# Loading q and k of three start-up tiles by heads, in 2-KB rows, and turning them with 64x64 products

## The chip, the cores and the metric

The kernel runs on one core of a Trainium2 chip. The core has a matrix engine (PE in the rows; its weight loads stand apart as PEld), a vector engine (DVE), a scalar engine (ACT), GpSimd (POOL) and SyncE (SP), which here only issues transfers. Sixteen DMA engines move the data of all transfers. The metric is the device time of one execution in microseconds; lower is better.

## The reference, cut to what matters

```python
def _attn_ref(q, k, v):                       # each (8, 8, 576, 64): batch, head, token, dim
    chunk = 64                                # attention within chunks of 64 tokens
    scores = scale * np.matmul(q_c, k_c.transpose(0, 1, 2, 4, 3))
    scores = scores - np.max(scores, axis=-1, keepdims=True)
    attn = np.exp(scores)
    attn = attn / (np.sum(attn, axis=-1, keepdims=True) + 1e-09)
    return np.matmul(attn, v_c)
...
def _moe_ref(x, w_in, w_out, g_ln):           # x: 4608 tokens x 512 (8 heads x 64)
    h = x @ w_in                              # 512 x 1024
    e = np.exp(h - np.max(h, axis=-1, keepdims=True))
    solu = h * (e / (np.sum(e, axis=-1, keepdims=True) + 1e-09))
    ln = (solu - mean) / np.sqrt(var + 1e-06) * g_ln
    return (ln @ w_out).astype(np.float32)    # 1024 x 512
```

The weights come as 8-byte numbers; q, k and v are 4-byte. A token of one head is 64 numbers, 256 bytes, and eight tokens of one head that follow each other lie together in memory (2 KB).

## The kernel before, in words

The 4608 tokens are cut into 36 tiles of 128 tokens (two chunks of 64). For each tile the kernel needs q and k turned, so that the 64 dims of a head lie on partitions: the tiles qT and kT, each 128 partitions (two heads x 64 dims) by four head pairs by 128 tokens. From them PE makes the scores (sx), DVE subtracts the maximum (s_nmax, then e), ACT takes the exponential, DVE sums and divides (s_sum, s_rinv, s_e), the result is turned (attn_t) and multiplied with v. That gives x, already turned, and x goes as a high and a low part (x_h, x_l) into the first product (ph, 24 products of 512 columns), through the softmax and the normalisation (z), and as z_h and z_l into the second product (po, 24 more).

From tile 5 on the tiles run through a loop that is the same for each. Before it stands a start-up whose order is written out by hand, in the table `START` (lines 18 to 31). Each word is a step of a tile or of a piece of weight: `n:1` loads q and k of tile 1, `N:1:0` and `N:1:1` turn its q and its k (the first time the word stands the products are issued, the second time the copy out of PSUM), `S:1` makes its scores, `P:1` loads weight piece 1 (1 MB), `c`, `b`, `C`, `t` and `d` convert a weight piece from 8-byte numbers to a high and a low part on POOL, DVE and ACT, and `w:6` puts six products with the identity on PE, whose results nobody reads. Each engine takes its instructions in the order in which the words stand. `MOVED` says which copies go to DVE and which conversions to POOL; the copies of the turned q and k of tiles 1 to 3 are on ACT.

Tiles 0 to 8 are loaded by `load_natural` (line 317) into the buffer `nat`, which has two places; tile i uses place i % 2. A token lies on a partition and its eight heads side by side. `turn_natural` (line 333) turns a tile with four 128x128 transposes for q and four for k, each taking two heads. All these loads, and the loads of the weights and of v, are issued by SP on one queue. Up to eight are under way, since an issue waits for the one eight places before it, and a load into `nat` also waits until PE has turned the tile that lay in that place.

Of the kernel before, what the change touches and what calls it, by code (L numbers as in the profile page):

```python
# [62 lines left out]
def chunk_attention_then_solu_ffn(  # L63
# [12 lines left out]
    B, H, S, D = q.shape  # L76
    DM, FF = H * D, g_ln.shape[0]
    P = 128
    CH = 64
    NCH = S // CH  # L80
    HP = H // 2
# [25 lines left out]
    def po():  # L107
# [10 lines left out]
    pe, dve, act, pool, sync = (  # L118
        order.engine(e)
        for e in (nc.tensor, nc.vector, nc.scalar, nc.gpsimd, nc.sync)  # L120
    )
# [3 lines left out]
    def evict(word, to, of):  # L125
        if word in moved:
            dve.tensor_copy(out=to, in_=of)
        else:
            act.copy(to, of)

    def bank():
        return ps_t.tile([P, FF // 2], F32, name="tp")

    ident = const.tile([P, P], F32, name="ident")
# [111 lines left out]
    QT, KT, V, QS, KS = {}, {}, {}, {}, {}  # L246
# [19 lines left out]
    def qk_tiles(i):  # L266
        QT[i] = work.tile([P, HP, P], F32, name="qT")
        KT[i] = work.tile([P, HP, P], F32, name="kT")
# [19 lines left out]
    def chunk_of(i, c):  # L288
        n = 2 * i + c
        return n // NCH, n % NCH  # L290
# [17 lines left out]
    nat = work.tile([P, 2, 2, H, D], F32, name="nat", tag="z_t")  # L308

    def tile_parts(i):  # L310

        (b0, n0), (b1, n1) = chunk_of(i, 0), chunk_of(i, 1)
        if b0 == b1:
            return [(0, P, b0, n0 * CH)]
        return [(0, CH, b0, n0 * CH), (CH, P, b1, n1 * CH)]

    def load_natural(i):

        for x, src in enumerate((q, k)):
            for p0, p1, b, s in tile_parts(i):  # L320
                sync.dma_start(
                    nat[p0:p1, i % 2, x],
                    src[b, :, s:s + p1 - p0, :].rearrange("h t d -> t h d"),
                )
# [8 lines left out]
    def turn_natural(i, x):  # L333
        if i not in QT:
            qk_tiles(i)
        t = nat[:, i % 2, x]
        pt = bank().rearrange("p (a t) -> p a t", t=P)
        for hp in range(HP):
            pe.transpose(
                pt[:, hp, :],  # L340
                t[:, 2 * hp:2 * hp + 2, :].rearrange("p a d -> p (a d)"),
                ident,
            )
        yield
        evict(f"N:{i}:{x}", (QT, KT)[x][i], pt)
# [8 lines left out]
    def attn(i):  # L354
        return sy if order.on and i % 2 else sx
# [20 lines left out]
    def softmax_a(i):  # L376
        sv = attn(i)[:, :, 0].rearrange("p j a k -> p a j k")
        nmax = small.tile([P, HP, 2], F32, name="s_nmax")
        dve.tensor_reduce(
            out=nmax, in_=sv, axis=AX.X, op=ALU.max, negate=True  # L380
        )
        e = ES[i % 2][:, :, :CH]
        dve.tensor_tensor(
            out=e.rearrange("p (a j) k -> p a j k", j=2), in0=sv,
            in1=nmax.unsqueeze(3).to_broadcast([P, HP, 2, CH]), op=ALU.add,
        )
        st[i, "e"] = e
# [80 lines left out]
    def start_softmax(i):  # L468
        softmax_a(i)
        yield  # L470
        softmax_e(i)
# [270 lines left out]
    def warm(n):  # L742
# [6 lines left out]

    todo = {  # L750
        "P": load_pair, "n": load_natural,
        "v": load_v, "g": load_g, "Q": load_batch, "q": load_some,
        "G": scale_g, "N": turn_natural, "S": scores, "A": start_softmax, "B": softmax_b,
        "T": attn_transpose, "U": attn_turn, "V": start_values, "c": unit_scale,
        "b": unit_bits, "C": unit_join, "t": unit_high, "d": unit_low, "M": ffn_in, "X": solu_a, "Y": solu_b,
# [19 lines left out]
    for i in range(first, NT):  # L775
# [36 lines left out]
        if odd:  # L812
            if i + 3 < NT:
                softmax_a(i + 3)
                softmax_e(i + 3)
            if i + 1 < NT:
                x_high(i + 1)
        elif i + 1 < NT:
            x_low(i + 1)
# [25 lines left out]
        if odd and i + 4 < NT:  # L845
            softmax_a(i + 4)
# [34 lines left out]
```

## Time and profile before

| | us |
|---|---|
| median of 3 runs | 472.41 (471.82 to 473.7) |
| the profiled execution: time | 473.01 |
| the profiled execution: span of its instructions | 471.2 |

| engine | busy, share of the span |
|---|---|
| PE | 98% |
| PE weight loads | 81% |
| DVE | 79% |
| ACT | 54% |
| POOL | 31% |

A share of the whole span is a mean over two different stretches. The start-up takes about 88 us of the 471; the loop takes the rest. So each stretch is read by itself: first a table of busy times by stretch, then each engine's instructions in order of time. In these, an instruction that stood idle before it has the idle time and what ended it in brackets, and an instruction without brackets followed the one before it on its engine without a gap.

### The profile page before, as it was taken

To read this page: it belongs to the slowest core of one execution; us is meant where nothing else is said; L and a number is where in the kernel's file an instruction comes from. 1 tells how busy PE (TensorE), PEld (TensorE's weight loads), DVE (VectorE), ACT (ScalarE), POOL (GpSimd) and SP (SyncE) were. 2 spreads that over 40 slices of the span, in tenths; PEclk is the share of its full clock that TensorE was granted. 3 is DMA by queue.
4 is the path that set the end of the run, shared out by engine and by line. 5 is a ranking of instruction groups with operands and counts; after the bars stand their busy time and mean duration, and the time that the engine had idled before them with its cause. 6 is when DMAs were issued, how large, how long until landed. Compare 5 with 4: busy or idle time off the path is not lost.

```text
span 471.2 us, 11062 instructions
## 1 busy us (share of the span) xinstructions
PE 461.9 (98%) x4212; PEld 380.9 (81%) x4212; DVE 374.1 (79%) x521; ACT 256.4 (54%) x422; POOL 147.6 (31%) x298
## 2 busy tenths in 40 slices
PE   8999999999999999999999999999999999999997
PEld 6677778788888888888888888888888888888886
DVE  3999999797869887878788878797979797954441
ACT  2979984555544646464645455554555554545451
POOL 2212716151505050505050505042514141424430
PEclk9999999999999999999999999999999999999999
DMA  9999999878786878687258496948743535343231
GB/s 244 313 278 217 216 138 179 176 184 150 194 140 170 154 181 162 167 154 177 70 144 167 134 175 157 180 126 173 160 112 105 121 91 136 85 118 96 73 95 50
DMA packets 192924, 72.57 MB, mean 154 GB/s; under 512 B 177188, under 2 KB 177960, under 8 KB 191976
## 3 DMA queue, kind: packets, MB, share of 16 engines
q1 hardware_dynamic: 186200, 58.89, 57.3%
q0 software_dynamic: 6528, 12.86, 10.3%
q8 instruction: 33, 0.54, 0.5%
q14 instruction: 19, 0.16, 0.1%
q10 hardware_dynamic: 144, 0.13, 0.1%
HBM read 36.70 MB, written 9.44 MB: 98 GB/s over the span
## 4 chain that ended last, share of the span: by engine, by line
PE 85%; DMA 5%; DVE 3%; ACT 3%; SPq 2%; issue 1%; DVEq 0%; ACTq 0%
PE po L54 39%; PE ph L54 37%; PE tp L54 5%; PE sx L54 4%; SPq L54 2%; DMA nat<-in_q_dram 2%; DMA v_sb<-in_v_dram 2%; ACT z L54 1%; DMA attn_t<-a_b 1%; ACT attn_t L54 1%; ACT wo_h L54 1%; DVE z_b L54 1%; DVE z L54 0%; DVE s_sum L54 0%; ACT sq L54 0%
## 5 line engine op out<-in xcount | busy, mean ns | idle before, releaser
L54 ACT ACTIVATE z<-ph,h_nmax 128x1024 f32<-128x1024 f32 x36 | 40.2, 1118 | 139.1 <-DVE h_nmax L54 139.1
L54 PE MATMUL po<-wo_l,z_h 128*128 128x512 f32 (+1 forms) x288 | 113.0, 392 | 0.0
L54 PE MATMUL ph<-wi_l,x_h 128*128 128x512 f32 x288 | 112.8, 392 | 0.0
L54 PE MATMUL ph<-wi_h,x_h 128*128 128x512 f32 x288 | 112.2, 389 | 0.0
L54 PE MATMUL po<-wo_h,z_l 128*128 128x512 f32 (+1 forms) x288 | 111.6, 388 | 0.0
L54 PE MATMUL po<-wo_h,z_h 128*128 128x512 f32 (+1 forms) x288 | 111.4, 387 | 0.0
L54 POOL DMA_DIRECT2D z_t<-z_b x144 | 71.8, 506 | 27.0 <-DVE z_b L54 21.9
L54 PE MATMUL ph<-wi_h,x_l 128*128 128x512 f32 x288 | 78.1, 390 | 0.0
L54 POOL TENSOR_TENSOR u<-ssq,eps 128x1 f32<-128x1 f32 x36 | 6.8, 189 | 213.3 <-ACT sq L54 213.1
L54 DVE TENSOR_REDUCE h_nmax<-ph 128x1 f32<-128x1024 f32 x36 | 44.0, 1222 | 31.3 <-PE ph L54 31.2
L54 PEld LDWEIGHTS ph<-wi_h,x_l 128*128 128x128 f32 x288 | 53.9, 188 | 11.6 <-DVE x_l L54 0.4
L54 PEld LDWEIGHTS po<-wo_l,z_h 128*128 128x128 f32 x288 | 54.1, 188 | 11.4
L54 PEld LDWEIGHTS ph<-wi_l,x_h 128*128 128x128 f32 x288 | 54.1, 188 | 11.5 <-ACT x_h L54 0.2
L54 PEld LDWEIGHTS po<-wo_h,z_l 128*128 128x128 f32 x288 | 54.1, 188 | 11.1
L54 PEld LDWEIGHTS ph<-wi_h,x_h 128*128 128x128 f32 x288 | 54.1, 188 | 11.0
L54 PEld LDWEIGHTS po<-wo_h,z_h 128*128 128x128 f32 x288 | 54.1, 188 | 10.5
L54 DVE TENSOR_TENSOR z_l<-z_t,z_h 128x1024 fp32r<-128x1024 f32 (+1 forms) x37 | 42.0, 1136 | 20.9 <-ACT z_h L54 17.7
L54 DVE SCALAR_TENSOR_TENSOR z<-ph,z 128x1024 f32<-128x1024 f32 x36 | 44.1, 1224 | 13.3 <-ACT z L54 13.2
L54 ACT ACTIVATE z<-z,z_sum 128x1024 f32<-128x1024 f32 x33 | 38.1, 1155 | 22.9 <-DVE z L54 21.7
L54 DVE STREAM_TRANSPOSE z_b<-z 128x1024 f32<-128x1024 f32 x34 | 41.2, 1212 | 7.2 <-DMA v_sb<-in_v_dram 3.3
L54 ACT CAST z_h<-z_t 128x1024 fp32r<-128x1024 f32 (+1 forms) x37 | 36.0, 972 | 8.5 <-PE po L54 4.9
L54 ACT ACTIVATE o_sb<-po,r 128x512 f32<-128x512 f32 (+1 forms) x36 | 24.3, 674 | 24.7 <-POOL r L54 18.6
(76 smaller groups left out, 589.8 us busy)
## 6 DMA issues: line engine op xcount, KB each, us to landing
out_dram<-o_sb SPq DMA_DIRECT2D x35, 256.0 KB, 2.5
v_sb<-in_v_dram SPq DMA_DIRECT2D x32, 256.0 KB, 4.3
z_t<-z_b POOLq DMA_DIRECT2D x128, 64.0 KB, 2.8
z_t<-z_b SPq DMA_DIRECT2D x128, 64.0 KB, 3.0
q_st<-in_q_dram SPq DMA_DIRECT2D x96, 72.0 KB, 3.3
k_st<-in_k_dram SPq DMA_DIRECT2D x96, 72.0 KB, 3.1
w_raw<-in_moe_w_out_dram SPq DMA_DIRECT2D x4, 1024.0 KB, 7.5
attn_t<-a_b POOLq DMA_DIRECT2D x60, 64.0 KB, 3.8
```

The source lines that it names most:

```text
L54: ins = make(*args, **kwargs)
```

## The change

q and k of tiles 1, 2 and 3 are loaded another way. A partition now takes eight tokens of one head, which are 2 KB in one piece: partition 16h + g has tokens 8g to 8g + 7 of head h. The source of the load is walked as 8 heads of 16 rows of 512 numbers; before it was walked as 128 tokens of 8 heads of 64 numbers. A load is 128 rows of 2 KB, before 1024 rows of 256 bytes.

The turn becomes sixteen 64x64 products with the identity for q and sixteen for k. A product takes one of the eight token places of four heads (64 partitions). Its result is 64 dims by 64 columns (four heads x 16 groups of eight tokens), and the copy out of PSUM puts the columns back into the order of the tokens: it reads the eight tokens of a group 64 numbers apart. Row half j of head pair a now has head 4j + a, before 2a + j, and the subtraction that writes e puts the heads back in order.

```diff
+    BY_HEADS = (1, 2, 3)
+
     def load_natural(i):
 
+        if i in BY_HEADS:
+            (_, _, b, s), = tile_parts(i)
+            for x, src in enumerate((q, k)):
+                sync.dma_start(
+                    nat[:, i % 2, x].rearrange("p h d -> p (h d)"),
+                    src[b, :, s:s + P, :].rearrange("h (g t) d -> h g (t d)", t=8),
+                )
+            return
...
         t = nat[:, i % 2, x]
+        if i in BY_HEADS:
+            pt = bank()
+            for y in range(8):
+                for j in range(2):
+                    half = slice(j * D, (j + 1) * D)
+                    pe.matmul(
+                        pt[half, y * D:(y + 1) * D], t[half, y, :], ident[half, half],
+                        start=True, stop=True,
+                    )
+            yield
+            evict(
+                f"N:{i}:{x}", (QT, KT)[x][i].rearrange("p a (g t) -> p a g t", t=8),
+                pt.rearrange("p (t a g) -> p a g t", t=8, a=HP),
+            )
+            return
...
-            out=e.rearrange("p (a j) k -> p a j k", j=2), in0=sv,
+            out=e.rearrange(
+                "p (j a) k -> p a j k" if i in BY_HEADS else "p (a j) k -> p a j k", j=2
+            ),
+            in0=sv,
```

On SP, at the start of the program, the order of the loads is as follows (nat is the buffer of q and k, w_raw a weight piece; the numbers are the shape of the destination):

```order
 L54 DMA g_in<-in_moe_g_ln_dram 4x256
 L54 DMA w_raw<-in_moe_w_in_dram 128x1024 x2
-L54 DMA nat<-in_q_dram 128x8x64
-L54 DMA nat<-in_k_dram 128x8x64
+L54 DMA nat<-in_q_dram 128x1x512
+L54 DMA nat<-in_k_dram 128x1x512
 L54 DMA w_raw<-in_moe_w_in_dram 128x2048
 L54 DMA v_sb<-in_v_dram 128x8x64
 L54 DMA w_raw<-in_moe_w_in_dram 128x2048
```

No load moves in the order; the two of tile 1 change shape, and so do those of tiles 2 and 3 behind them.

On PE, the turns of tile 1 stand between products with the identity (ph<-ident), ahead of the scores of tile 1 (sx<-kT,qT):

```order
 L54 MATMUL ph<-ident 128x256 x3
-L54 MATMUL tp<-ident,nat 128x128 x4
+L54 MATMUL tp<-ident,nat 64x64 x16
 L54 MATMUL ph<-ident 128x256
-L54 MATMUL tp<-ident,nat 128x128 x4
+L54 MATMUL tp<-ident,nat 64x64 x16
 L54 MATMUL ph<-ident 128x256
 L54 MATMUL sx<-kT,qT 64x64 x16
```

Here too nothing moves; each group of four becomes sixteen in its place. The order on DVE, ACT and POOL is the same as before.

## Rows read from the trace of the kernel before

**Rows 1.** Busy us by stretch: PE, PEld, DVE, ACT, POOL; clock, DMA share, GB/s.
```profile
18.00:24.00 6.00, 5.58 (x59) 4.21 (x58) 5.90 (x10) 5.44 (x9) 1.88 (x2) 1.00 1.04 284
24.00:30.00 6.00, 5.71 (x63) 4.43 (x62) 5.90 (x9) 4.88 (x8) 0.28 (x1) 1.00 0.96 219
30.00:54.00 24.00, 23.47 (x299) 19.20 (x298) 23.25 (x34) 20.55 (x41) 9.90 (x7) 1.00 0.97 261
54.00:78.00 24.00, 23.33 (x195) 18.77 (x196) 23.09 (x33) 16.22 (x30) 9.87 (x16) 1.00 1.05 143
...
100.00:460.00 360.00, 360.00 (x3183) 298.14 (x3182) 285.94 (x397) 185.70 (x299) 113.54 (x244) 1.00 0.62 140
```

**Rows 2.** The chain that ended last, in order of time: start, length, what.
```profile
9.84 9.55 DMA nat<-in_q_dram
...
19.43 0.66 PE tp L54 x4
```

**Rows 3.** DVE in order of time: start, length, instruction, idle before and its end.
```profile
13.59 0.69 DVE L54 TENSOR_REDUCE s_nmax<-sx 128x8 f32<-128x512 f32 x1 [0.52 <-PE sx L54]
...
21.83 1.22 DVE L54 SCALAR_TENSOR_TENSOR w_a<-w_a,w_b 128x1024 uint32<-128x1024 uint32 x1
22.97 0.69 DVE L54 TENSOR_REDUCE s_nmax<-sx 128x8 f32<-128x512 f32 x1
...
28.74 0.68 DVE L54 TENSOR_REDUCE s_nmax<-sx 128x8 f32<-128x512 f32 x1
...
53.80 0.69 DVE L54 TENSOR_REDUCE s_nmax<-sx 128x8 f32<-128x512 f32 x1 [0.44 <-ACT x_h L54]
...
65.09 1.22 DVE L54 SCALAR_TENSOR_TENSOR z<-ph,z 128x1024 f32<-128x1024 f32 x1 [0.51 <-ACT z L54]
```

**Rows 4.** ACT in order of time, start-up.
```profile
10.75 1.06 ACT L54 ACTIVATE w_a<-w_a 128x1024 f32<-128x1024 f32 x1 [0.95 <-POOL w_a L54]
11.72 0.57 ACT L54 COPY qT<-tp 128x512 f32<-128x512 f32 x1
12.18 0.59 ACT L54 COPY kT<-tp 128x512 f32<-128x512 f32 x1
...
18.05 1.17 ACT L54 CAST wi_h<-w_a 128x1024 fp32r<-128x1024 f32 x1
...
21.13 0.59 ACT L54 COPY kT<-tp 128x512 f32<-128x512 f32 x1 [0.42 <-PE tp L54]
```

**Rows 5.** PE in order of time, the turns and scores of tiles 1 to 3.
```profile
11.11 0.63 PE L54 MATMUL tp<-ident,nat 128*128 128x128 f32 x4
...
12.82 0.69 PE L54 MATMUL sx<-kT,qT 64*64 64x64 f32 x32 [0.66 <-ACT kT L54]
...
19.43 0.66 PE L54 MATMUL tp<-ident,nat 128*128 128x128 f32 x4 [0.19 <-DMA nat<-in_q_dram]
...
20.44 0.66 PE L54 MATMUL tp<-ident,nat 128*128 128x128 f32 x4
...
21.77 0.69 PE L54 MATMUL sx<-kT,qT 64*64 64x64 f32 x32 [0.24 <-ACT kT L54]
...
25.25 1.11 PE L54 MATMUL tp<-ident,nat 128*128 128x128 f32 x8
...
27.76 0.69 PE L54 MATMUL sx<-kT,qT 64*64 64x64 f32 x32
```

**Rows 6.** The same columns as rows 1: two stretches of 256-byte rows, one of 8-KB rows.
```profile
2.00:4.00 2.00, 2.00 (x6) 1.35 (x4) 0.00 (x0) 0.01 (x1) 0.00 (x0) 1.00 1.09 236
...
35.50:37.50 2.00, 2.00 (x10) 1.64 (x10) 2.00 (x3) 1.90 (x7) 1.10 (x1) 1.00 1.06 200
42.00:44.00 2.00, 1.89 (x41) 1.57 (x40) 2.00 (x3) 1.74 (x4) 0.00 (x0) 1.00 1.01 397
```

**Rows 7.** DMA issues up to 26 us: KB each, median us from issue to landing.
```profile
nat<-in_k_dram SPq DMA_DIRECT2D x4, 256.0 KB, 7.1
...
g_in<-in_moe_g_ln_dram SPq DMA_DIRECT2D x1, 4.0 KB
```

## The prediction

> **What bounds the kernel now.** I read the busy times by stretch first. From 100 to 460 us PE is busy 360.00 of 360.00 us, so the loop is bound by PE, and a delay or a gain of the start-up is handed on to the end whole. In the start-up another engine is full: from 18 to 78 us DVE is busy 5.90, 5.90, 23.25 and 23.09 us of 6, 6, 24 and 24, which is 58.1 of 60 [rows 1]. The DMA engines are loaded too (shares of 0.96 to 1.05), and so is PE, but part of PE's work there is filler.
>
> Then I read the chain of waits. It goes through 9.55 us of the load of q of tile 2 and on to its turn [rows 2]. That would make the loads look like the bound. But the row of that turn on PE says that PE had stood idle for 0.19 us only [rows 5]: up to then it ran fillers, which can't start earlier. The chain shows what ended last at each step, not how much an earlier end would give.
>
> So I read DVE in order of time. Its last sizeable wait of the early start-up is at 13.59 us, 0.52 us for the scores of tile 1. Behind that it goes without a gap to 53.80 (0.44 us), and then to 65.09 (0.51 us) [rows 3]. A change of the loads moves the end by what it does to DVE at the three places where DVE takes scores of tiles 1, 2 and 3: 13.59, 22.97 and 28.74 us. These places are where the sum is made.
>
> **Loads, the price.** Stretches with 256-byte rows alone move 200 and 236 GB/s; one with 8-KB rows moves 397 [rows 6]. By engine (a sixteenth) that is 17.4 to 20.5 ns for a 256-byte row and 330 ns for an 8-KB row. A load of 1024 short rows is 64 to an engine, so 1.11 to 1.31 us, 1.2 in the middle. No stretch has 2-KB rows from memory alone. On the line between the two sizes a 2-KB row takes 20.5 + 309.5 x 1792/7936 = 90 ns. The bounds are 83 ns (a quarter of an 8-KB row) and 164 ns (eight 256-byte rows).
>
> What a load then takes depends on how its 128 rows are dealt out. Over all 16 engines it is 8 rows each, 0.72 us, 0.5 us less than before. Over eight it is 16 each, 1.45 us, some 0.2 us more than before. The source is now walked as 8 heads of 16 rows; before it was walked as 128 tokens. The nearest row is that of g_in, the only load whose outermost count is small (4): it is also the only one of the group for which the profile gives no landing time [rows 7]. I read this as its not having been counted in like the others, which fits a load that runs on fewer engines. It is weak evidence, yet it is the only row on the point, so I take eight engines. Loads of a queue keep their order on each engine, so those eight fall behind by 0.2 us with every such load, and each later load, which needs all 16, lands when they do: tile 1 lands 0.4 us later, tile 2 0.8, tile 3 1.2.
>
> The page "DMA: Bandwidth & Descriptors" of the Trainium skill (section "Why a DMA increments its semaphore by 16 and not by 1") states that a transfer runs on the largest number of engines up to 16 that divides the slowest dimension of both its patterns. By that this load has eight engines, which is the sum made here; with sixteen it would be the first rival. No view here names the engine of a packet.
>
> **Turns, the price.** Sixteen 64x64 products with the same shape as the scores take 0.69 us; four transposes take 0.63 to 0.66 [rows 5]. I take 0.1 us more for each turn, with the change of shape before and behind it; the bounds are 0 and 0.3. The copies stay on ACT at 0.57 to 0.59 us [rows 4]; they now read numbers 64 apart. I take no change, and keep the price for a rival. The other order in which e is written is the same number of elements in runs of 64: nothing. On SP the six issues have fewer rows to hand over; nothing behind them gets ahead of the data of the 16 engines, so this gives nothing.
>
> **The sum, at the three places.**
> Tile 1: k's turn starts at 11.11 and ends at 11.74; the copy of k starts at 12.18, since ACT first ends w_a (from 10.75) and the copy of q (from 11.72) [rows 4, 5]. So 0.44 us of slack take the 0.4 us of lateness, and 0.1 us of the longer turn is left: about 0.05 us at 13.59.
> Tile 2: k's turn at 20.44 becomes 21.24 by the load, and ends 0.9 us later with the longer product run; the copy of k at 21.13 waits for it and the scores at 21.77 for the copy [rows 4, 5]. They end at 22.46 now and would end at 23.36. DVE takes them at 22.97, when it has ended w_a [rows 3]. Slack of 0.51: DVE is 0.4 us late.
> Tile 3: both turns run from 25.25 to 26.36, and the scores at 27.76 follow behind the products between them without idle time [rows 5]. The load of k was just in time, so 1.2 us of lateness and 0.2 us of two longer turns put the end of the scores from 28.45 to 29.85. DVE takes them at 28.74 [rows 3], slack 0.29: 1.1 us late, the 0.4 us of tile 2 within it.
> Behind that DVE has no gap in which to win this back before 53.80, and the gaps there are waits for ACT, which follows DVE. I take 1.0 us to the end. On the profiled execution: 471.2 of span and 1.8 around it are 473.0, and 474.0 after. That execution was 0.6 us above the median of the runs, 472.41; so the forecast is 473.4 us. Its own range is 472.2 (rows of 83 ns, 236 GB/s not reached before) to 474.7 (rows of 100 ns: 0.4 us late with each load, 2.4 by tile 3, 2.3 behind the slack).
>
> **Rivals.**
> 1. All 16 engines: the loads do get faster, 0.5 us each, tile 3 lands 3 us earlier, and it is hidden. For it: the destination has 128 partitions as before. What comes earlier is taken by fillers and by ACT's conversion at 10.75 [rows 4], and DVE is full. The turns cost PE 0.2 us ahead of the scores of tile 3. 472.6 us.
> 2. Slower: the strided copies. If reading 64 apart doubles the 0.58 us of a copy, both copies of tile 1 stand one behind the other ahead of the scores: 1.2 us at 13.59, of which the 0.44 us of slack is no cover, since ACT itself is the late one. The copies of tile 3 follow DVE's work on tile 2 through ACT's exponential, so they start that late too and end up to 1.2 us later still, less the 0.29 us of slack at 28.74: 2.1 us in all, 474.5, or 475.5 on top of the eight engines. The nearest row is the CAST at 18.05, which reads every other number and takes 1.17 us where a plain activation takes 1.06 [rows 4]: a tenth more, 0.06 us a copy. It decides over the eight engines from 0.5 us a copy, where the two of tile 1 cost the 1.0 us of the forecast. The Trainium skill's page "PSUM — Partial Sum Buffer" (section "Specifications (TRN2)") says that PSUM has lines of 8 bytes and that a pattern that isn't contiguous slows matmuls a lot. If copies were slowed like that, the price would be this rival's. No row here shows a copy that reads PSUM in steps of single numbers.
> 3. Slower still: eight engines and dear rows. At 110 ns a row a load is 0.56 us late, 3.4 by tile 3, and 3.3 at the end with the longer turns and the slack: 475.7. At the bound of 164 ns it would be 7 us and more.
> 4. Faster: the loads are the bound after all, as the chain has it. DVE's idle time from 13 to 78 us in the rows is 0.52, 0.44 and 0.51 us [rows 3], so even with all of it gone the gain is 1.5 us, 470.9.
>
> **How the numbers follow.** Eight engines 0.53, sixteen 0.22, strided copies 0.08, dear rows 0.13, faster 0.04. A measurement can tell some 0.5% from no change, 2.4 us, so faster is below 470.05 and slower above 474.77. Of the first case 0.06 lies above that, and half of the strided copies. Slower: 0.06 + 0.04 + 0.13 = 0.23. Faster: 0.02 of the last case. Same: 0.75. The range goes from 471.6, which leaves out most of the last rival, to 475.8, just above the third; beyond it lie rows nearer to the upper bound and two slower cases at once.
>
> **What would show it.** Landing times of q and k of tile 3 later than before: eight engines; three us earlier: sixteen. The rows of qT<-tp and kT<-tp for tiles 1 to 3 at 0.59 us: copies free. Sixteen products in 0.69 us. DVE's takes at 13.59, 22.97 and 28.74 moved by 0.05, 0.4 and 1.1, and the same shift of 1.0 kept at 65 us. I am wrong if DVE wins the time back, if the granted clock, 1.00 in every stretch of before, falls while PE waits longer for tiles 2 and 3, or if the first place moves by more than 0.5.

## The result and the profile after

| | before | after |
|---|---|---|
| median of the runs on one chip | 472.18 us (471.82 to 473.7, 4 runs) | 477.39 us (477.06 to 478.19, 4 runs) |
| span of the profiled execution | 471.2 us | 476.4 us |

The ratio is 1.0107 (95% interval 1.008 to 1.0133). The change made the kernel 5.2 us slower. Forecast were 473.4 us and "no change" as the likeliest, with a range to 475.8: the time lies outside.

First the busy times by stretch after the change, in the columns of [rows 1], with two stretches that [rows 1] doesn't have (12 to 18 and 78 to 90).

```profile
12.00:18.00 6.00, 5.08 (x102) 4.03 (x99) 2.89 (x4) 2.81 (x5) 1.15 (x1) 1.00 1.07 336
18.00:24.00 6.00, 6.00 (x84) 4.67 (x82) 5.88 (x10) 5.53 (x9) 1.27 (x1) 1.00 0.66 230
...
78.00:90.00 12.00, 12.00 (x87) 9.81 (x86) 11.19 (x17) 6.41 (x12) 7.64 (x16) 1.00 0.89 217
100.00:460.00 360.00, 360.00 (x3183) 298.23 (x3182) 289.30 (x402) 185.99 (x300) 115.15 (x248) 1.00 0.63 140
```

The loop is the same: 360.00 of 360.00 us on PE, clock 1.00. What was lost lies ahead of it. From 12 to 18 us DVE is busy for only 2.89 us of the 6; in before it was 5.40:

```profile
12.00:18.00 6.00, 5.34 (x84) 4.38 (x84) 5.40 (x7) 5.46 (x10) 1.68 (x2) 1.00 1.13 332
```

And the last two columns say what the transfers do: from 18 to 24 us the sixteen DMA engines are busy for 0.66 of the time on the mean, where they were at 1.04 [rows 1], and yet the load of k of tile 3, issued at 15.43, lands only at 31.2 (the chain below). A load is late while a third of the engines' time is free. The packets of the trace (a packet is one row of a load, and the views show only their sums) say why. The 2-KB rows of tiles 1, 2 and 3 are moved from 7.07 to 12.83, from 18.36 to 22.93 and from 23.90 to 30.04 us, and in 98% of the time in which any of them is moved, no more than nine are moved at once: as eight engines give it, with some overlap of the records.

PE in order of time, the turns and scores of tiles 1 to 3, as in [rows 5] (x32 stands for 16 products, since each shows as two instructions).

```profile
11.61 1.15 PE L54 MATMUL tp<-ident,nat 64*64 64x64 f32 x32 [1.50 <-DMA nat<-in_q_dram]
...
14.25 1.15 PE L54 MATMUL tp<-ident,nat 64*64 64x64 f32 x32 [0.87 <-DMA nat<-in_k_dram]
...
16.08 0.69 PE L54 MATMUL sx<-kT,qT 64*64 64x64 f32 x32
...
24.14 1.15 PE L54 MATMUL tp<-ident,nat 64*64 64x64 f32 x32
25.22 0.66 PE L54 MATMUL tp<-ident,s_e 128*128 128x128 f32 x4
...
29.57 1.15 PE L54 MATMUL tp<-ident,nat 64*64 64x64 f32 x32
31.32 1.15 PE L54 MATMUL tp<-ident,nat 64*64 64x64 f32 x32 [0.60 <-DMA nat<-in_k_dram]
...
33.99 0.69 PE L54 MATMUL sx<-kT,qT 64*64 64x64 f32 x32
```

Two things are to be seen. A turn takes 1.08 to 1.15 us (behind the one at 24.14 the next instruction starts after 1.08), not 0.69. And k of tile 1 is turned at 14.25 where it was at 11.11 [rows 5], behind a wait for its load; k of tile 3 at 31.32, again behind its load, where the eight transposes of q and k ran from 25.25 to 26.36 with no wait. The chain of waits has the two loads as its longest pieces (start, length, what):

```profile
4.34 9.78 DMA nat<-in_k_dram
14.12 0.14 issue
14.25 1.15 PE tp L54 x32
15.40 0.03 PE ph L54
15.43 15.75 DMA nat<-in_k_dram
```

DVE in order of time, as in [rows 3]:

```profile
16.84 0.69 DVE L54 TENSOR_REDUCE s_nmax<-sx 128x8 f32<-128x512 f32 x1 [3.08 <-PE sx L54]
...
26.76 0.69 DVE L54 TENSOR_REDUCE s_nmax<-sx 128x8 f32<-128x512 f32 x1 [0.46 <-PE sx L54]
...
34.75 0.69 DVE L54 TENSOR_REDUCE s_nmax<-sx 128x8 f32<-128x512 f32 x1 [1.82 <-PE sx L54]
...
71.80 1.23 DVE L54 SCALAR_TENSOR_TENSOR z<-ph,z 128x1024 f32<-128x1024 f32 x1 [0.51 <-ACT z L54]
...
88.15 1.23 DVE L54 STREAM_TRANSPOSE z_b<-z 128x1024 f32<-128x1024 f32 x1
...
99.51 0.65 DVE L54 TENSOR_REDUCE s_nmax<-tp 128x8 f32<-128x512 f32 x1
```

The takes of the scores moved by 3.25, 3.79 and 6.01 us, forecast 0.05, 0.4 and 1.1. At the z of 65.09 the shift is 6.71, but at the s_nmax of 99.51 it is 4.61: some 2 us are given back in between. Two rows of before lie further on than the prediction read:

```profile
84.86 1.25 DVE L54 STREAM_TRANSPOSE z_b<-z 128x1024 f32<-128x1024 f32 x1 [3.33 <-DMA v_sb<-in_v_dram]
...
94.90 0.65 DVE L54 TENSOR_REDUCE s_nmax<-tp 128x8 f32<-128x512 f32 x1
```

DVE stood idle for 3.33 us there, and after the change it reaches that instruction (88.15) without a wait, so the shift is 3.29 there. But it doesn't stay so small: it is 4.61 at 94.90 and 5.21 at the next z of before, 102.21 (107.42 after), which is the shift of the whole span. What the end keeps is decided on PE. PE has one wait in before between 78 and 100 us, and none after the change (12.00 of 12.00 us from 78 to 90, above):

```profile
84.00:90.00 6.00, 4.88 (x139) 3.90 (x139) 5.09 (x6) 2.55 (x4) 0.00 (x0) 1.00 1.00 231
```

```profile
86.59 0.96 PE L54 MATMUL sx<-attn_t,v_sb 64*64 64x64 f32 x29 [1.09 <-DMA attn_t<-a_b]
```

The copies that read numbers 64 apart are where the prediction had them, at 0.59 us as in [rows 4], for all of tiles 1 to 3:

```profile
15.44 0.59 ACT L54 COPY kT<-tp 128x512 f32<-128x512 f32 x1 [2.05 <-PE tp L54]
...
25.36 0.59 ACT L54 COPY kT<-tp 128x512 f32<-128x512 f32 x1 [1.12 <-PE tp L54]
```

### The profile page after: what moved, and what is told of

Its sections match the earlier page's. It is cut to its first block, busy times and chain, and to the rows that moved or that the text cites. A ratio compares the mean times of both kernels' runs of the same rounds, so it can differ in the third digit from the quotient of the medians.

```text
span 476.4 us, 11400 instructions
## 1 busy us (share of the span) xinstructions
PE 466.5 (98%) x4380; PEld 385.1 (81%) x4380; DVE 376.3 (79%) x521; ACT 256.2 (54%) x422; POOL 147.1 (31%) x298
## 4 chain that ended last, share of the span: by engine, by line
PE 86%; DMA 5%; DVE 5%; ACT 2%; SPq 1%; issue 0%; DVEq 0%; ACTq 0%
PE po L54 41%; PE ph L54 37%; DMA nat<-in_k_dram 5%; PE tp L54 4%; PE sx L54 4%; DVE wo_l L54 1%; DVE z L54 1%; SPq L54 1%; DVE h_nmax L54 1%; ACT attn_t L54 1%; DVE w_a L54 0%; ACT w_a L54 0%; DVE w_b L54 0%; DVE e L54 0%; ACT wo_h L54 0%
```

## The experiments

The medians are of runs on one chip for the first four experiments (before: 472.13 us) and for the other four (before: 472.21 us).

| kernel | median, us | ratio to before, 95% interval | shift of DVE's takes of tiles 1, 2, 3, us | shift of z at 65.09 | shift of s_nmax at 94.90 | shift of the span |
|---|---|---|---|---|---|---|
| the change | 477.39 | 1.008 to 1.0133 | 3.25, 3.79, 6.01 | 6.71 | 4.61 | 5.2 |
| e1, loads alone, eight heads outermost | 476.23 | 1.0054 to 1.0111 | 2.57, 2.57, 4.38 | 5.10 | 2.99 | 3.6 |
| e2, turns alone | 474.69 | 1.0033 to 1.0069 | 0.40, 0.94, 2.35 | 2.97 | 2.14 | 2.7 |
| e3, loads with sixteen groups outermost, and turns | 475.18 | 1.0037 to 1.0075 | 2.09, 2.64, 4.04 | 3.98 | 1.88 | 2.5 |
| e4, loads alone, sixteen groups outermost | 472.94 | 0.9986 to 1.0027 | 0.84, 0.85, 0.99 | 1.37 | -0.17 | 0.1 |
| e5, turns alone, one corner at a time | 478.24 | 1.0112 to 1.0157 | 2.39, 4.39, 7.12 | 7.52 | 5.43 | 6.0 |
| e6, the change for tile 1 alone | 474.52 | 1.0029 to 1.0071 | 2.33, 2.34, 2.33 | 2.86 | 1.13 | 1.7 |
| e7, the change for tile 3 alone | 475.37 | 1.0053 to 1.0093 | -0.03, 0.16, 2.00 | 1.96 | 1.66 | 1.8 |
| e8, loads alone, in two of four heads | 485.24 | 1.026 to 1.0312 | 5.62, 7.96, 11.82 | 13.09 | 10.97 | 11.7 |

The shifts are of one profiled execution each, so a few tenths of a microsecond say nothing in them.

**The loads alone (e1).**

```diff
 def turn_natural(i, x):
-        if i in BY_HEADS:
+        if i in ():
...
-                "p (j a) k -> p a j k" if i in BY_HEADS else "p (a j) k -> p a j k", j=2
+                "p (a j) k -> p a j k", j=2
```

> The loads by heads alone; q and k of tiles 1 to 3 are still turned with four 128x128 transposes, which mixes heads and tokens of these tiles, so only the time is of use. Theory A (each load by heads runs on eight of the 16 DMA engines and holds back everything behind it): most of the 5.2 us stay, +3.5 to +4.5 over the kernel before, 476 to 477. Theory B (the sixteen products are what costs, the late loads are covered): +0 to +0.7, 472.2 to 472.9. Theory C (rows of 2 KB are dear on however many engines): as A here.

476.23 us, 4.1 above before, as theories A and C had it: the loads alone are the larger part of the loss. A part of the 4.1 may be PE's clock. In the profiled execution PE waited 2.54 us for q of tile 1, and from 12 to 18 us its granted clock had a mean of 0.75 (1.00 in the change); the transposes of tile 1 took 1.09 to 1.12 us instead of 0.63 to 0.66. The three of the seven runs with a granted clock of 1.000 over the whole have a median of 475.3, 3.2 above before. In the stretch from 18 to 24 us the DMA engines' share falls to 0.62, and tile 3's k is waited for:

```profile
18.00:24.00 6.00, 5.87 (x60) 4.30 (x58) 5.89 (x9) 5.45 (x8) 1.20 (x1) 1.00 0.62 202
```

```profile
30.42 0.63 PE L54 MATMUL tp<-ident,nat 128*128 128x128 f32 x4 [1.32 <-DMA nat<-in_k_dram]
```

**The turns alone (e2).**

```diff
 def load_natural(i):
-        if i in BY_HEADS:
+        if i in ():
```

> The sixteen products and the strided copies alone; q and k are loaded by tokens as before, so heads and tokens of tiles 1 to 3 are mixed and only the time is of use. In the trace of the changed kernel a turn takes 1.15 us where four transposes took 0.63 to 0.66, so 0.5 us more each, two for each tile. Theory A: +0.5 to +1.5 (472.7 to 473.7), since the slack of 0.3 to 0.5 us at each tile takes part of it. Theory B: +4 to +5, about 477.

474.69 us, 2.6 above before: more than theory A allowed (to 473.7) and less than theory B. PE goes on without a wait from the turns of tile 1 to the scores of tile 3, so the longer turns add up there: the scores of tile 2 start at 23.15, not 21.77, which is 1.38 us late. Tile 3's two turns start 1.48 us later than in [rows 5] and take 2.08 us where the eight transposes took 1.11; the scores start at 30.33, not 27.76, and DVE, which had 0.29 us of slack there, takes them 2.35 us late:

```profile
26.73 2.08 PE L54 MATMUL tp<-ident,nat 64*64 64x64 f32 x64
...
30.33 0.69 PE L54 MATMUL sx<-kT,qT 64*64 64x64 f32 x32
```

**The same rows on sixteen engines (e3 with the turns, e4 without).** The source is walked as sixteen groups of eight heads. The rows, their 2 KB and their number are the same, and only the partition on which each lands is another.

```diff
-                    src[b, :, s:s + P, :].rearrange("h (g t) d -> h g (t d)", t=8),
+                    src[b, :, s:s + P, :].rearrange("h (g t) d -> g h (t d)", t=8),
```

> The changed kernel with one edit: the source of the load is walked as 16 groups of 8 heads, so partition 8g + h has the group g of head h. The same rows of 2 KB, the same products and copies; heads and tokens of tiles 1 to 3 are mixed, so only the time is of use. Theory A: the loads now run on 16 engines and land earlier than in the kernel before; what is left is the price of the turns, +0.5 to +1.5 (472.7 to 473.7). Theory B: as changed, 477. Theory C: as changed, 476 to 477.

> As the run before, and turned with four 128x128 transposes: the loads of 2-KB rows on 16 engines alone; heads and tokens of tiles 1 to 3 are mixed, so only the time is of use. It shows what faster loads are worth. Theory A, with DVE as the bound of the start-up: the loads land some 3 us earlier by tile 3 and nothing comes of it, -0.5 to +0.2 (471.7 to 472.4). If the loads were the bound, -2 to -3 (469 to 470). Theory C: +3.5 to +4.5.

With the transposes of before the loads now cost nothing that can be measured at the end: 472.94 us. With the new turns the time is 475.18 (to 473.7 were expected), which is 0.5 above the turns alone, with intervals that overlap. The DMA engines' share from 18 to 24 us is back at 1.03:

```profile
18.00:24.00 6.00, 5.75 (x60) 4.35 (x59) 5.93 (x9) 5.26 (x10) 1.15 (x1) 1.00 1.03 278
```

In the packets up to eighteen rows of 2 KB are moved at once, and more than ten in 40% of the time in which any is. So neither the 2-KB rows nor the reading by heads cost 4 us; the eight as the outermost count did. But the loads didn't become faster, as I had expected. In e4 q and k of tile 1 land 7.0 and 7.4 us after their issue (6.4 and 6.9 in before), those of tile 3 at 25.2 and 26.4 us (24.1 and 25.6), and DVE's takes are 0.84 to 0.99 us late:

```profile
10.66 0.66 PE L54 MATMUL tp<-ident,nat 128*128 128x128 f32 x4 [1.40 <-DMA nat<-in_q_dram]
```

So no run here has faster loads, and the fourth rival, the loads as the bound, isn't tested; DVE's full rows alone speak against it. Why rows that are eight times as long don't land earlier stays open.

**One corner at a time (e5, on the turns alone).**

```diff
-            for y in range(8):
-                for j in range(2):
+            for j in range(2):
+                for y in range(8):
```

> The turns alone are changed (loads by tokens as before), and of their sixteen products the eight of the upper half of the rows now stand ahead of the eight of the lower half, so that neighbours share one corner of the array; the numbers come out in mixed places, as in the turns alone. Corner theory: products in different corners run side by side, and the rows so far are 0.62 us for sixteen over four corners and 1.08 over two; over one corner at a time it is then 16 x 0.135 = 2.1 us a turn, 1.0 us more than with the turns alone. Tile 3's scores come 3 us later still, and the end is 2 to 3 us above the 474.7 of the turns alone: 477 us. Rival, a product of 64x64 costs 68 ns whatever its neighbours (load of weights, issue): a turn stays at 1.15 us in the rows and the time at 474.7.

478.24 us (477 were expected). With the very same sixteen products in another order a turn takes 1.70 to 1.90 us (64 instructions, two turns, in 3.40), where 2.1 were expected:

```profile
10.19 1.90 PE L54 MATMUL tp<-ident,nat 64*64 64x64 f32 x32
...
30.16 3.40 PE L54 MATMUL tp<-ident,nat 64*64 64x64 f32 x64
```

A fixed price for a product would have left it at 1.15. The scores, whose neighbours go round all four corners (both halves of the rows and both of the columns), take 0.62 to 0.69; the turn, in which a half of the rows always goes with the same half of the columns, has two corners and takes 1.08 to 1.15; with one it takes 1.7 to 1.9. The page "TensorEngine Tiling (Array Packing)" of the Trainium skill (section "Key Properties") states that the tiles of the array work independently; the three rows agree. From two corners to one only the order changes. From four to two something else changes too: in the kernel the scores write the two halves of the rows to two stretches of PSUM of 512 numbers a partition each, and a turn writes both to the same one. No run separates the two, and a turn over four corners wasn't tried.

**Tile 1 alone and tile 3 alone (e6, e7).**

```diff
-    BY_HEADS = (1, 2, 3)
+    BY_HEADS = (1,)        # e6;  (3,) in e7
```

> The whole change, for tile 1 alone; tiles 2 and 3 are loaded and turned as before. Theory 'kept': what tile 1 loses stays, since the queue keeps its order and the vector engine is full behind it. The shift at its three takes of scores is +3.2, +3.3, +3.3 us, +3.3 at 65 us, and some 1.5 us are absorbed where it waits at 81 to 85 us: span +1.8, 474.0 us. Rival 'won back': the loads of tile 3 alone set the start-up, tile 1's delay is taken up by the slack ahead of tiles 2 and 3: shift +3.2, then below 1, end +0.3: 472.5 us. Rival 'by thirds': each tile adds a third of 5.2: 473.9.

> The whole change, for tile 3 alone. Theory 'kept': nothing moves at the first two takes; at the third the two loads are 1 us late each and the two turns take 1.0 us more together, less 0.3 us of slack: +2.7 us, the same at 65 us, of which some 1.5 are absorbed behind it: 473.3 us. Rival 'won back': the third take alone sets the end, so nearly all of the loss is here: +5, 477 us. Rival 'by thirds': 473.9.

Tile 1's delay stays: 2.33, 2.34 and 2.33 us at the three takes, and 2.86 at z. That is "kept" (2.3 for 3.2 in size); "won back" is refuted from both sides, since tile 3 alone gives 2.00 at its take and not 5. The two rows of e6 that carry it:

```profile
15.92 0.69 DVE L54 TENSOR_REDUCE s_nmax<-sx 128x8 f32<-128x512 f32 x1 [2.19 <-PE sx L54]
...
67.95 1.23 DVE L54 SCALAR_TENSOR_TENSOR z<-ph,z 128x1024 f32<-128x1024 f32 x1 [0.51 <-ACT z L54]
```

For tile 3 alone the way is another than I expected. PE doesn't wait for its loads; what comes late is a weight piece, for which DVE waits 0.69 us, and the turns are longer. The piece stands ahead of them in the queue (issued at 13.59, they at 17.2 and 18.1) and lands 11.6 us after its issue, 9.5 in before. So not only transfers behind the loads by heads come late:

```profile
25.23 0.69 DVE L54 TENSOR_SCALAR w_b<-w_raw 128x1024 uint32<-128x1024 uint32 x1 [0.69 <-DMA w_raw<-in_moe_w_in_dram]
...
30.74 0.68 DVE L54 TENSOR_REDUCE s_nmax<-sx 128x8 f32<-128x512 f32 x1
```

The medians, 474.52 and 475.37, don't tell "kept" from "by thirds" for tile 1, the shifts of the span (1.7 and 1.8) are a third of 5.2 each, and the median of tile 3 is 2 us above "kept" (473.3). Its profiled execution (474.78 us) is among the shortest of its six (474.64 to 476.27) and doesn't show the rest; that stays open.

**Two loads of four heads (e8, on the loads alone).**

```diff
-                sync.dma_start(
-                    nat[:, i % 2, x].rearrange("p h d -> p (h d)"),
-                    src[b, :, s:s + P, :].rearrange("h (g t) d -> h g (t d)", t=8),
-                )
+                for c in range(2):
+                    sync.dma_start(
+                        nat[c * D:(c + 1) * D, i % 2, x].rearrange("p h d -> p (h d)"),
+                        src[b, 4 * c:4 * c + 4, s:s + P, :].rearrange("h (g t) d -> h g (t d)", t=8),
+                    )
```

> The loads alone (transposes as before, so heads and tokens come out mixed, as in the loads alone), but each load is cut into two of four heads, 64 rows of 2 KB each. Theory: a load runs on as many engines as its outermost count divides, and always from the same first one. Then both halves lie on the same four engines, 32 rows each: at 134 ns (the 5.7 us that the loads alone were late at tile 3's turns over 6 loads, and 1.2 us of a load before, over 16 rows) 4.3 us a load where it was 1.2, 18 us late by tile 3, and 488 us at the end. Rival: the halves go to different engines, eight in all: as the loads alone, 476.2. Rival: it isn't the engines but the reading by heads that is slow: as the loads alone, 476.2, with both halves of a load spread alike.

485.24 us: 13 above before, where the loads alone were 4.1. The halves don't spread over two sets of engines, which would have left it at 476.2: in the packets no more than five rows of 2 KB are moved at once in 99% of the time in which any is. From 24 to 30 us, with loads of tile 3 issued and not landed, the sixteen engines are busy for a third of the time on the mean, and behind that PE waits for k of tile 3:

```profile
24.00:30.00 6.00, 3.47 (x29) 2.41 (x31) 5.64 (x8) 3.36 (x5) 0.00 (x0) 1.00 0.33 107
```

```profile
37.85 0.63 PE L54 MATMUL tp<-ident,nat 128*128 128x128 f32 x4 [2.39 <-DMA nat<-in_k_dram]
```

The size was over-forecast. k of tile 3 is turned at 37.85, and in before at about 25.8 (the second half of the eight transposes from 25.25): 12 us late over six loads, 2.0 a load instead of 3.1. In this profile PE also stood idle and its granted clock fell to a mean of 0.58 in the stretch from 12 to 18 us, which is mostly the lower of its two levels (1.2 of 2.4 GHz; e1's mean was 0.75 there, that of the change 1.00). So a part of its first shift is a slower PE.

## Why the prediction was wrong

**The bound, right as far as it was tested.** In before DVE sets the start-up, and a delay at one of its takes stays: 2.33, 2.34 and 2.33 us in e6. With the change PE joins it: from 18 to 24 us PE is busy 6.00 of 6.00 us, and DVE waits for the scores at all three takes (3.08, 0.46 and 1.82 us). That faster loads would gain nothing is not shown, since e4's weren't faster; the 3 us that the first rival gave them at tile 3 didn't come.

**Eight engines, right; the price of it, wrong.** This is the step that failed: "Over eight it is 16 each, 1.45 us, some 0.2 us more than before." The mechanism was the one that happened (e1 against e4, e8, and the rows moved at once), but the term was mis-sized by a factor of four to eight. k of tile 1 is turned 3.1 us late after two loads, 1.6 a load; k of tile 3 is turned at 31.32 instead of about 25.8, 5.5 us over six loads, 0.9 a load. With 1.2 us for a load of before and 16 rows to an engine that is (1.2 + 1.6) / 16 = 175 ns a row at tile 1 and (1.2 + 0.9) / 16 = 131 ns over all six, both estimates. The packets give the row itself: 128 ns on the mean in the change (146, 102 and 136 for tiles 1, 2 and 3), where the sum had 90. With 16 rows to an engine that is 2.0 us a load, and with 64 rows of 256 bytes at 21.6 ns, as in before, 1.4: 0.7 late and not 0.2. The rest of the 0.9 isn't traced. The 90 ns came from a line drawn between two stretches in which all sixteen engines moved data. The upper bound of 164 ns stood in the prediction, but its range ended at rows of some 110 ns. Rival 3 (eight engines and dear rows) was the case, with 475.7 at 110 ns.

**What the lateness meets, half right.** At tile 1 the slack of 0.44 us was meant to take all of 0.4; against 3.1 it is nothing. Loads behind a late one are late too, as the prediction had it. But a weight piece that stands ahead of the loads by heads comes late as well (e7), which the order that the prediction assumed doesn't give, and which the sum left out.

**The turns, wrong in size.** "Sixteen 64x64 products with the same shape as the scores take 0.69 us": the shape is the same, the corners are not. A turn costs 0.5 us more than four transposes, not 0.1, and lies outside the bounds of 0 to 0.3. Six of them alone cost 2.6 us (e2), where the sum had 0.1 for each: the second term that was mis-sized.

**The two together** cost less than their sum (4.1 and 2.6 against 5.2). In the rows of PE after the change the turn of q of tiles 1 and 3 lies ahead of a wait for k (0.87 and 0.60 us), so q's longer turn can be hidden by k's load there.

**Copies and the order of e, right.** 0.59 us in every copy. The second rival falls. The Trainium skill's rule on patterns that aren't contiguous (page "PSUM — Partial Sum Buffer", section "Specifications (TRN2)") speaks of matmuls, and these copies don't show it.

**Handed on whole, wrong.** I read DVE to 78 us and took the shift to the end as it was. In every kernel of the table the shift shrinks between z at 65.09 and s_nmax at 94.90, by 0.3 to 2.1 us, and the span keeps all but 0.2 to 1.5 us of the shift at z. Most of it goes into PE's wait at 86.59. From 84 to 90 us PE is idle for 1.12 us in before; 0.93 of it is left in e2 and 0.92 in e7, where 0.3 and 0.2 us of the shift are lost, and 0.05 or less in the others, where 1.2 to 1.5 are; the 0.1 to 0.4 beyond PE's idle time aren't traced. That is why e4's 1.37 us ends as nothing. Had I had the right 6.7 us, I would have forecast 479 and not 477.4. DVE's idle time of 3.33 us at 84.86 is no measure of it. Which transfer ends that idle time is not settled: the rows put it down to the load of v in before, e2 and e4, and to others in e6 and e7.

## What to carry to other kernels

Before changing the shape of a load, look at its outermost count: 2-KB rows with eight as the outermost count were slower than 256-byte rows with 128, and the transfers around them came late with them; the sign in the profile is a DMA share well under 1 while someone waits for a load. Price small products by the row of a kernel that uses the same corners of the array, not merely the same shape. And follow a delay up to the stretch that is bound by another engine: here most of what was won back went into the idle time that this engine still had there.

## What the runs showed of the hardware

- The same 128 rows of 2 KB by an outermost count of 16, 8 and 4 (the last in two loads): 472.94, 476.23 and 485.24 us.
- At most nine of these rows were moved at once in 98% of the time with eight as the outermost count (the change), at most five in 99% with two loads of four (e8), and up to eighteen with sixteen (e4).
- A row of 2 KB had no fixed price. By the packets its mean was 146, 102 and 136 ns for tiles 1, 2 and 3 in the change, 132 in e4 and 104 in e8; a row of 256 bytes of the same loads in before (tiles 1 and 2) took 21.6. By the lateness of k of tile 3 the estimates are 131 ns in the change and (1.2 + 2.0) / 32 = 100 in e8. Why the price varies wasn't tested.
- Sixteen 64x64 products took 0.62 to 0.69 us over four corners, 1.08 to 1.15 over two and 1.70 to 1.90 over one. Whether the second stretch of PSUM that the four-corner products write has a part in it wasn't tested.
